# Batch 1's first transform step: pairs of pieces on 64x64 parts of the array, at other places of batch 0's group steps

## The chip, the cores and the metric

The kernel runs on one core of one Trainium2 chip. The metric is the device time of one execution in microseconds (us); three executions of the kernel before are given, and one more was profiled.

## The reference

The input `x` has 8 batches of 3008 tokens with 256 channels. Every batch goes through a spectral filter along its tokens (a real transform, a product with a complex filter, the transform back), and the result through a SwiGLU block with 1536 hidden units.

```python
X = np.fft.rfft(x, axis=1)
y = np.fft.irfft(X * (filt_r + 1j * filt_i)[None], n=x.shape[1], axis=1)
z = y.reshape(8 * 3008, 256)
g = z @ w_gate
out = (g * (1.0 / (1.0 + np.exp(-g))) * (z @ w_val)) @ w_out
```

All arrays here are 32-bit floats; the weights arrive as 64-bit floats and are rounded to 32 bits by the kernel itself while batch 0 is worked on.

## The kernel before

**The transform.** 3008 is 47 times 64, and the filter is worked out in steps of short transforms: over 47 values (`N1`), of which 24 complex outputs (`NS`) are kept, and over 64 (`N2`). The first step of batch 1 is the method `stage1` of the class `Spectral`. It works on 16 pieces (`N_ONE`) of `NV` = 2 token columns. A piece holds, on 94 partitions, the 47 rows of each of two halves (`h` = 0 and 1, token 32h + n of every row of 64), interleaved; the table `wf_t` (94 x 96) does both halves in one matmul, with zeros where the halves would mix. So a piece is one matmul of 94 x 96 on 512 columns into a PSUM bank, one copy by ScalarE (ACT) into a tile `t1`, and one store from the ACT queue into the DRAM tile `d1`, from which the next step (`stage2a`, first loads in `load_two`) reads. The inputs are loaded by `load_x` from SyncE's queue (SP), two DMAs a piece (80 and 14 rows), into the pool `xp` with two buffers: the first two pieces are loaded ahead, and piece u + 2 is asked for right after the matmul of piece u. `t1` has two buffers as well.

**Banks.** Of the eight PSUM banks, one belongs to the pool `fps` (function `fbank`), seven to `wps` (`NB` = 7, function `bank`). The group steps below take their accumulators from `wps`; `stage1` of batch 1 takes `fps` alone. A new `wps` tile gets the bank that was released first; its first writer waits until the last reader of the tenant before has ended.

**The group steps.** A batch is 12 steps (4 chunks of tokens by 3 groups of hidden units). Each step is one `Group`, and runs through one list of about 230 tokens, `SCHEDULE`, written out by hand; every instruction keeps this program order on its engine. Tokens such as `Q0` or `A13` are matmul pairs into the banks `k0` to `k3`, `a..` and `e..` (in the profile `wk`, `wa`, `we`; `W` tokens are the output products, `wA`, `wF`, `wG`). `f`, `c`, `m`, `g`, `u` are ACT's, `s`, `x`, `y`, `e`, `l`, `h`, `v` are mostly VectorE's (DVE) with some of ACT, `D` and `S` GpSimd's (POOL). A token with `'` belongs to the step before.

**Where the pieces go.** A token `tN.M` calls `next` once on entry N of the step's list `plan[step]`; a piece that is a generator runs to its next `yield`. The parts of the list that matter here:

```python
Q0 o3' z1.o' t4.2' W2 b0 f0 S00' S01' ... t0.0 x1.o' i1 Q1 t0.1 x2.o' P3 x3.o' f1 t4.3'
W1 x4.o' S10' x03 S11' D01 ... s13 b3 x5.o' P1 o1 b4 t0.2 P0 o2 z0.o c1 i5 A13 ...
... B01 h13 o7 t1.3 t2.0 s02 s12 g01 h2 b5 Q3 t2.1 h01 e12 A02 y23 W4 e02 ... A12 o4 z2.o t2.2 E12
... u13 E23 t3.2 m03 v13 E01 l23 e03 t3.3 t4.0 l01 u23 B23 v23 u01 E03 n1 t4.1 v01 g23 B03
```

Before the change `plan[0]`, `plan[1]` and `plan[2]` hold the four `stage3` pieces of batch 0 and one `stage1` piece each, at `t4`; `plan[3]` and `plan[4]` hold five pieces each, `plan[5]` three. Steps 6 to 10 hold `stage2a` and `stage2b` of batch 1. In steps 0 to 9 the rounding of the weights (`Preparation`, called `preparation.tick`) runs at further places between the tokens, on DVE, ACT and POOL.

In the profiled execution steps 0 to 5 lie at about 75 to 260 us. A step's `t4` is near its end, `t0` soon after its start, `t2` in its middle.

Of the kernel before, what the change touches and what calls it, by code (L numbers as in the profile page):

```python
# [41 lines left out]
FP32 = mybir.dt.float32  # L42
# [6 lines left out]
B, S, C = 8, 3008, 256  # L49
# [4 lines left out]
N1, N2 = 47, 64  # L54
# [71 lines left out]
def dft_tables():  # L126
    n1, n2 = np.arange(N1), np.arange(N2)
    s, q = np.arange(NS), np.arange(NQ)
    ph = 2 * np.pi * (np.outer(n1, s) % N1) / N1
    w = np.stack([np.cos(ph), -np.sin(ph)], 1)  # L130
    wf = np.zeros((N1, 2, NS, 2, 2))
    wi = np.zeros((NS, 2, 2, N1, 2))

    v = np.stack([2 * np.cos(ph), -2 * np.sin(ph)], 0)
    v[0, :, 0], v[1, :, 0] = 1.0, 0.0
    for h in range(2):
        wf[:, h, :, :, h] = w.transpose(0, 2, 1)
        wi[:, :, h, :, h] = v.transpose(2, 0, 1) / S
    one = wi[:, :, 0, :, 0].transpose(1, 0, 2).reshape(2 * NS, N1)
    back = np.zeros((128, 10 * N1))  # L140
    for tile_, first in zip(BACK, BACK_AT):
        for i, (_, row, a, rows) in enumerate(tile_):
            back[row:row + rows, first + N1 * i:first + N1 * (i + 1)] = one[a:a + rows]


    kap = np.where(q[:, None] < 32, s + N1 * q[:, None], s + N1 * (95 - q[:, None]))
    sg = np.where(q < 32, 1.0, -1.0)[:, None]
    th = 2 * np.pi * ((n2[:, None, None] * kap) % S) / S
    c, sn = np.cos(th), np.sin(th)
    d = np.zeros((2, N2, NS, 2, NQ))  # L150
    d[0, :, :, 0] = c.transpose(0, 2, 1)
    d[1, :, :, 0] = sn.transpose(0, 2, 1)
    d[0, :, :, 1] = (-sn * sg).transpose(0, 2, 1)
    d[1, :, :, 1] = (c * sg).transpose(0, 2, 1)
    d = d.reshape(128, NS, 128)
    chunks = np.arange(128).reshape(2, 2, NCHUNK, NW).transpose(2, 0, 1, 3).ravel()
    de = np.stack([d, d.transpose(2, 1, 0)[:, :, chunks]], 2)

    hi = 2 * np.pi * (np.outer(2 * n1 + 1, s) % (2 * N1)) / (2 * N1)
    scale = np.where(s == 0, 1.0, 2.0) / S  # L160
    one_hi = np.concatenate([np.cos(hi) * scale, -np.sin(hi) * scale * (s > 0)], 1).T
    for tile_, first in zip(BACK, BACK_AT):
        for i, (n, row, a, rows) in enumerate(tile_):
            if n >= NH:
                back[row:row + rows, first + N1 * i:first + N1 * (i + 1)] = one_hi[a:a + rows]

    quad = np.zeros((4, 32, 2, 32))
    for h in range(2):
        turn = 2 * np.pi * (np.outer(2 * n1[0:NS] + h, s) % (2 * N1)) / (2 * N1)
        quad[2 * h:2 * h + 2, 0:NS, 0, 0:NS], quad[2 * h:2 * h + 2, 0:NS, 1, 0:NS] = np.cos(turn), -np.sin(turn)  # L170
        quad[2 * h:2 * h + 2, 23 * h] *= np.array([0.5, 0.0])[:, None]
    quad = np.concatenate([quad.reshape(128, 64), np.tile([[1.0], [-1.0]], (64, 1))], 1)

    four = np.zeros((128, N_FOUR + 1, 2, 4, 64))
    lo, qq = np.arange(32), np.arange(32)
    for t in range(NS):
        u, at = divmod(t, 4)
        for e in range(2):
            qa = np.where(qq < 16, 2 * qq, 62 - 2 * (qq - 16)) + e
            ang = 2 * np.pi * (np.outer(lo, t + N1 * qa) % S) / S  # L180
            cs, sn, sign = np.cos(ang), np.sin(ang), np.where(qa < 32, 1.0, -1.0)
            there = np.stack([np.stack([cs, -sn * sign], 2), np.stack([sn, cs * sign], 2)], 0)
            part = 64 * (at // 2)
            four[part:part + 64, u, 0, at % 2 * 2 + e] = there.reshape(64, 64)
            home = np.stack([np.stack([cs.T, sn.T], 2),
                             np.stack([-(sn * sign).T, (cs * sign).T], 2)], 1)
            four[64 * e:64 * e + 64, u + 1, 1, at] = home.reshape(64, 64)
    four = four.reshape(128, N_FOUR + 1, 2, 256)

    thc = th - np.where(n2 < 32, 0.0, 1.0)[:, None, None] * 2 * np.pi * s / (2 * N1)  # L190
    c, sn = np.cos(thc), np.sin(thc)
    turned = np.zeros((2, N2, NS, 2, NQ))
    turned[0, :, :, 0] = c.transpose(0, 2, 1)
    turned[1, :, :, 0] = sn.transpose(0, 2, 1)
    turned[0, :, :, 1] = (-sn * sg).transpose(0, 2, 1)
    turned[1, :, :, 1] = (c * sg).transpose(0, 2, 1)
    turned = turned.reshape(128, NS, 128).transpose(2, 1, 0)

    pairs = np.arange(128).reshape(2, N2).T.ravel()
    later = np.stack([de[:, :, 0], turned[:, :, pairs]], 2)  # L200
    f32 = np.float32
    return (wf.reshape(NR, NK).astype(f32), wi.reshape(NK, NR).astype(f32),
            back.astype(f32), quad.astype(f32), four.astype(f32), np.ascontiguousarray(de).astype(f32),
            np.ascontiguousarray(later).astype(f32))


# [1 line left out]
def kernel(  # L208
# [8 lines left out]
    out: bass.AP,  # L217
):
    nc = tc.nc
    wf_host, wi_host, back_host, quad_host, four_host, de_host, later_host = dft_tables()  # L220
    wf_dram = nc.inline_tensor(wf_host, name="wf_tbl")
    wi_dram = nc.inline_tensor(wi_host, name="wi_tbl")
    quad_dram = nc.inline_tensor(quad_host, name="quad_tbl")
    four_dram = nc.inline_tensor(four_host, name="four_tbl").ap()
    back_dram = nc.inline_tensor(back_host, name="back_tbl")
    de_dram = nc.inline_tensor(de_host, name="de_tbl").ap()
    later_dram = nc.inline_tensor(later_host, name="later_tbl").ap()
# [14 lines left out]

    wf_t = cpool.tile([NR, NK], FP32)
    wi_t = cpool.tile([NK, NR], FP32)

    wt_t = cpool.tile([128, NPR, 2, 128], FP32)
    y_t = cpool.tile([128, 3 * len(PAIRS), TQ], FP32)
# [32 lines left out]
    f_dram = wdpool.tile([128, 2, NS, C], FP32, name="filter")  # L280
    wo_t = cpool.tile([128, NJ, 7, 128], FP32)

    off_t = cpool.tile([128, 1], FP32)
    top_t = cpool.tile([128, 1], FP32)
    one = cpool.tile([128, 1], FP32)
    nc.vector.memset(off_t, -896.0)
    nc.vector.memset(top_t, 255.0)

# [303 lines left out]
    class Spectral:  # L592


        def __init__(self, b):
            self.b = b
            self.quads_dram, self.turned = quads_dram[b % 2], turned_dram[b % 2]
            self.d1, self.d2 = [dram_tiles[2 * (b % 2) + i] for i in range(2)]
            self.d1_rows = self.d1.rearrange("a (h n) c -> (a h) n c", h=2)

            self.d2_tokens = self.d2.rearrange("a n c -> (a n) c").rearrange(
                "(n a) c -> n a c", n=N2)
            flat = self.d2.rearrange("a n c -> (a n) c")
            self.d2_parts = flat.rearrange("(s q) c -> q s c", q=128)
            self.d2_rows = flat.rearrange("(s k a n) c -> k s a n c", k=NCHUNK, a=4, n=NW)
            self.rest = []
            self.x, self.t2, self.f, self.tb, self.p, self.t4, self.y = {}, {}, {}, {}, {}, {}, {}
            self.real = {}
# [13 lines left out]
        def load_x(self, u):  # L622
# [15 lines left out]
                        self.load(out=up[ts(n, 32)].rearrange("p (q c) -> p q c", c=C),  # L638
                                  in_=rows[0:32, first:first + 4])
            elif u < N_ONE:  # L640
                self.x[u] = xpool.tile([NR, NV, C], FP32, name=f"x_{self.b}_{u}", tag="x")
                rows = x[self.b].rearrange("(r n) c -> r n c", n=32)

                for r in (slice(0, 80), slice(80, NR)):
                    self.load(out=self.x[u][r], in_=rows[r, ts(u, NV), :])

        def load_two(self, u):
            if u < N_TWO:
# [249 lines left out]
                self.f.pop(w)  # L898
            self.load_filter(w + 1)

        def stage1(self, u):

            t1 = t1pool.tile([NK, NV, C], FP32, name=f"t1_{self.b}_{u}", tag="t1", bufs=2)
            ps = self.bank(f"pa_{self.b}_{u}")
            pin(nc.tensor.matmul(out=ps[0:NK], lhsT=wf_t, rhs=self.x.pop(u),  # L905
                                         start=True, stop=True))
            self.load_x(u + 2)
            yield
            pin(nc.scalar.copy(out=t1, in_=ps[0:NK]))
            pin(nc.scalar.dma_start(out=self.d1_rows[:, ts(u, NV), :], in_=t1))  # L910

        def stage1_first(self, u):

# [332 lines left out]
    def run(piece):  # L1246
        for _ in piece:
            pass

    with tc.tile_pool(name="start", bufs=1) as spool0:  # L1250
# [88 lines left out]
        idle(zero, [bank("idle") for _ in range(6)], 512)  # L1339
        for step in (0, 2, 1, 3):  # L1340
            run(spec.stage3(0, step))
        following = Spectral(1)
        for u in range(2):
            following.load_x(u)
# [86 lines left out]
    for b in range(B):  # L1431
# [5 lines left out]
            return [s.stage3(k, step) for step in range(4)]  # L1437

        d = [three(cur, k) for k in range(1, NCHUNK)]
        one = [] if b else [nxt.stage1(u) for u in range(N_ONE)]  # L1440
        bursts = [[] for _ in range(NCHUNK * NG)]
        if b and nxt:
            for n in range(N_QUAD // 2):
# [10 lines left out]
        if nxt:  # L1454
# [3 lines left out]
            plan[4], plan[7], plan[11] = d[1], [gap] + d[2], three(nxt, 0)  # L1458
            if b == 0:
                for k in range(NCHUNK - 1):  # L1460
                    plan[k] = d[k] + one[k:k + 1]
                plan[0] = [gap, d[0][0], chain(d[0][1], d[0][2]), d[0][3], one[0]]
                plan[3], plan[4], plan[5] = one[3:8], one[8:13], one[13:16]
                for n in range(5):
                    plan[6 + n] = two[5 * n:5 * n + 5]
                plan[6][0] = sooner(plan[6][0])
# [105 lines left out]
```

## Time and profile before

| what | value |
|---|---|
| median of 3 runs | 2815.08 us (2807.47 to 2815.55) |
| the profiled execution's own time | 2812.9 us |
| its span, first to last instruction | 2811.1 us |
| mean granted TensorE clock | 0.998 |
| PE (matmuls) busy | 2774.9 us, 99% |
| DVE, ACT, POOL busy | 2050.7, 1560.3 and 1580.6 us |
| matmul records of `stage1` of batch 1 (`pa`) | 32 for 16 matmuls, 590 to 595 ns each, from 100.5 to 248.2 us |
| its copies (`t<-pa`) | 16, 563 to 589 ns |
| its stores (`d<-t`) on the ACT queue | 16, 310 to 361 ns of that queue each |

How to read it: a matmul of 32-bit floats shows as two records of the whole width. PE is the matmul, PEld the load of its stationary operand, which lies beside it. Records overlap, so that the time which a matmul takes from its neighbours is the distance from its start to the start of what follows. A queue's DMA instruction (SPq, ACTq) is the time that the queue spends on issuing, not the transfer.

### The profile page before, as it was taken

How to read it: one execution, taken by the hardware profiler on the slowest of the kernel's cores; microseconds unless marked ns; L12 is line 12 of the kernel's file. 1: busy time of each engine (PE TensorE's matmuls, PEld its weight loads, DVE VectorE, ACT ScalarE, POOL GpSimd, SP SyncE). 2: the span in 40 equal slices, each digit the busy share in tenths (PEclk: the TensorE clock that was granted, in tenths of full speed). 3: DMA queues.
4: the chain of work that ended last, by engine and by line, in shares of the span. 5: the costliest groups of instructions: out<-in, count | busy, mean ns of one | idle time of the engine just before them, and what ended most of it. 6: DMA issues, size and time to landing. Idle time of an engine off the chain costs nothing.

```text
span 2811.1 us, 49259 instructions
## 1 busy us (share of the span) xinstructions
PE 2774.9 (99%) x15828; PEld 2310.4 (82%) x15828; DVE 2050.7 (73%) x4675; ACT 1560.3 (56%) x4170; POOL 1580.6 (56%) x1689
## 2 busy tenths in 40 slices
PE   8999999999999999999999999999999999999998
PEld 6877888788888888888888888888888888888887
DVE  7888767767677767777767677777677767666666
ACT  5775455555555555555555555555555555555554
POOL 5886576465545565456654566455555455545544
PEclk9999999999999999999999999999999999999999
DMA  9778877877676776677767776668766677654543
GB/s 215 234 262 278 286 237 233 261 233 268 187 214 207 249 243 193 206 233 227 245 187 227 217 247 221 204 193 257 243 209 204 212 237 229 190 153 147 153 138 82
DMA packets 385273, 608.53 MB, mean 216 GB/s; under 512 B 198877, under 2 KB 268445, under 8 KB 384841
## 3 DMA queue, kind: packets, MB, share of 16 engines
q1 hardware_dynamic: 366202, 574.39, 65.0%
q10 hardware_dynamic: 16174, 25.50, 3.5%
q0 software_dynamic: 2640, 5.51, 0.8%
q8 instruction: 128, 2.10, 0.3%
q14 instruction: 129, 1.05, 0.1%
HBM read 484.65 MB, written 118.12 MB: 214 GB/s over the span
## 4 chain that ended last, share of the span: by engine, by line
PE 91%; DVE 3%; POOL 2%; ACT 1%; DMA 1%; issue 0%; SPq 0%; POOLq 0%; ACTq 0%; DVEq 0%
PE wa L1123 25%; PE wk L1123 17%; PE wA L1220 17%; PE we L1123 12%; PE wG L1220 8%; PE wF L1220 4%; PE pd L1026 3%; PE wqc L823 1%; PE wqb L835 1%; PE wqa L743 1%; POOL h L323 0%; POOL out_dram L1205 0%; DMA lent<-later_tbl 0%; PE pc L980 0%; PE pa L905 0%
## 5 line engine op out<-in xcount | busy, mean ns | idle before, releaser
L1123 PE MATMUL wa<-y_t,wt_t 128*128 128x188 f32 x4464 | 882.4, 324 | 6.3 <-DVE wa L1145 4.6
L1123 PEld LDWEIGHTS wa<-y_t,wt_t 128*128 128x128 f32 x4464 | 748.4, 190 | 85.1 <-ACT wa L1149 9.5
L1123 PEld LDWEIGHTS wk<-y,wt_t 128*128 128x128 f32 x2976 | 494.6, 190 | 113.9 <-issue 34.0
L1123 PE MATMUL wk<-y,wt_t 128*128 128x188 f32 x2976 | 577.2, 326 | 1.8 <-ACT f L1138 1.3
L320 POOL TENSOR_TENSOR h<-h 128x376 f32<-128x376 f32 x190 | 182.7, 982 | 686.8 <-DVE h L1170 686.8
L323 POOL TENSOR_TENSOR h<-h 128x376 f32<-128x376 f32 x572 | 559.4, 999 | 15.4 <-DVE h L320 15.2
L1220 PE MATMUL wA<-h,wo_t 128*128 128x376 f32 x1532 | 550.6, 481 | 5.7 <-DVE o L320 2.1
L1123 PE MATMUL we<-y_t,wt_t 128*128 128x188 f32 x2232 | 433.0, 323 | 2.2 <-ACT we L1154 1.5
L323 POOL TENSOR_TENSOR D<-f,f 128x376 f32<-128x376 f32 x288 | 281.2, 987 | 246.4 <-ACT f L1138 231.2
L323 DVE TENSOR_TENSOR we<-we,m 128x376 f32<-128x376 f32 x576 | 319.2, 555 | 126.1 <-PE we L1123 60.7
L1123 PEld LDWEIGHTS we<-y_t,wt_t 128*128 128x128 f32 x2232 | 368.6, 190 | 6.2 <-DVE we L327 3.9
L1220 PEld LDWEIGHTS wA<-h,wo_t 128*128 128x128 f32 x1532 | 275.8, 190 | 113.5 <-POOL h L323 5.1
L1158 ACT COPY m<-wa 128x376 f32<-128x376 f32 x576 | 272.2, 473 | 84.1 <-PE wa L1123 80.1
L1165 ACT ACTIVATE u<-we 128x188 f32<-128x188 f32 x576 | 188.6, 327 | 173.0 <-DVE we L323 165.6
L1165 ACT ACTIVATE g<-wa 128x188 f32<-128x188 f32 x576 | 187.2, 325 | 165.0 <-PE wa L1123 157.5
L327 DVE SCALAR_TENSOR_TENSOR y<-wk,c 128x376 f32<-128x376 f32 x480 | 246.1, 539 | 40.5 <-ACT c L1142 23.0
L1220 PE MATMUL wG<-h,wo_t 128*128 128x376 f32 x768 | 274.0, 479 | 0.0
L1142 ACT COPY c<-wk 128x376 f32<-128x376 f32 x288 | 136.3, 473 | 212.7 <-PE wk L1123 212.6
L1154 ACT COPY we<-y 128x376 f32<-128x376 f32 x480 | 222.1, 480 | 18.8 <-DVE h L1170 14.0
L1138 ACT ACTIVATE f<-wk 128x376 f32<-128x376 f32 x288 | 139.8, 486 | 165.2 <-PE wk L1123 130.6
L1170 DVE TENSOR_TENSOR h<-wa,g 128x188 f32<-128x188 f32 x576 | 198.7, 346 | 34.4 <-ACT g L1165 34.2
L1170 DVE TENSOR_TENSOR h<-we,u 128x188 f32<-128x188 f32 x576 | 198.1, 344 | 29.0 <-ACT u L1165 17.6
(193 smaller groups left out, 3561.4 us busy)
## 6 DMA issues: line engine op xcount, KB each, us to landing
wt_t<-w_all SPq DMA_DIRECT2D x174, 896.0 KB
wt_t<-w_all SPq DMA_DIRECT2D x174, 768.0 KB
lent<-filter SPq DMA_DIRECT2D x36, 1024.0 KB
quads<-lent SPq DMA_DIRECT2D x96, 256.0 KB
d<-lent ACTq DMA_DIRECT2D x84, 256.0 KB
lent<-quads SPq DMA_DIRECT2D x144, 128.0 KB
lent<-raw SPq DMA_DIRECT2D x144, 128.0 KB
t<-d SPq DMA_DIRECT2D x114, 128.0 KB
```

The lines of the kernel that those rows point to most:

```text
L320: return eng.tensor_tensor(out=dst, in0=a, in1=b, op=ALU.add)
L323: return eng.tensor_tensor(out=dst, in0=a, in1=b, op=ALU.subtract)
L327: return nc.vector.scalar_tensor_tensor(out=dst, in0=a, scalar=-1.0, in1=b, op0=ALU.mult, op1=ALU.subtract)
L1026: pin(nc.tensor.matmul(out=rows, lhsT=self.t4[k, i][:, j, ts(cb, 128)], rhs=cols, start=j == 0, stop=True, skip_group_check=True))
L1123: pin(nc.tensor.matmul(out=ps[:, z], lhsT=self.wt[:, SLOT[p], z], rhs=rhs, start=start and z == 0, stop=True, skip_group_check=True))
L1138: pin(act.mul(self.small(f"f{i}", f"f{i}", 1), t[f"k{i}"], -1.0))
L1142: pin(act.copy(out=self.small(f"c{i}", f"c{i}", 1), in_=t[f"k{i}"]))
L1154: pin(act.copy(out=self.bank(f"e{at}"), in_=t[f"y{at}"]))
L1158: pin(act.copy(out=self.small(f"m{at}", "m", 4), in_=t[f"a{at}"]))
L1165: pin(act.activation(out=self.small(op, "g", 3, 1)[:, 0], in_=ps[:, 1], func=AF.Silu))
L1170: pin(v.tensor_tensor(out=dst, in0=ps[:, 0], in1=g, op=ALU.mult))
L1220: pin(nc.tensor.matmul(out=self.tiles[at], lhsT=wo_t[:, JB * q + i, WO[p], :], rhs=self.hs[i][:, HID[p]], start=start and i == 0, stop=Tru ...
```

## The change

Batch 1's `stage1` is called for 8 pairs v of pieces, 2v and 2v + 1. Half h of a piece lies on partitions 64h to 64h + 47 of a 128-partition tile (48 rows loaded, 47 used), two loads of 48 rows a piece. A table `both_t` (2 x 47 rows of 64 columns) replaces `wf_t` there. Each piece and half is a matmul of 47 x 64 on 512 columns on one quarter of the array: the half sets the rows of the array and the bank, the piece sets the columns and so the half of the bank's partitions. The pair's half 0 goes to the `fps` bank, its half 1 to a bank of `wps`. ACT copies both banks (128 x 512) in one part of the generator, and the four stores of 48 rows follow in a third part. The loads of the two pieces after next follow the four matmuls. The pairs are at `t4` of steps 1 and 2 (their stores at `t4.2'` of the step after) and at `t0` and `t2` of steps 3, 4 and 5; step 0 has none. `both_t` is loaded once from SP before the first loads of batch 1, and three one-column tiles become columns of one tile.

```diff
@@ load_x
-                self.x[u] = xpool.tile([NR, NV, C], FP32, name=f"x_{self.b}_{u}", tag="x")
-                rows = x[self.b].rearrange("(r n) c -> r n c", n=32)
-
-                for r in (slice(0, 80), slice(80, NR)):
-                    self.load(out=self.x[u][r], in_=rows[r, ts(u, NV), :])
+                self.x[u] = xpool.tile([128, NV, C], FP32, name=f"x_{self.b}_{u}", tag="x")
+                xb = x[self.b]
+                for h in range(2):
+                    self.load(out=self.x[u][64 * h:64 * h + 2 * NS],
+                              in_=bass.AP(tensor=xb.tensor, ap=[[N2 * C, 2 * NS], [1, NV * C]],
+                                          offset=xb.offset + (32 * h + NV * u) * C))
@@ stage1
-        def stage1(self, u):
-            t1 = t1pool.tile([NK, NV, C], FP32, name=f"t1_{self.b}_{u}", tag="t1", bufs=2)
-            ps = self.bank(f"pa_{self.b}_{u}")
-            pin(nc.tensor.matmul(out=ps[0:NK], lhsT=wf_t, rhs=self.x.pop(u),
-                                         start=True, stop=True))
-            self.load_x(u + 2)
-            yield
-            pin(nc.scalar.copy(out=t1, in_=ps[0:NK]))
-            pin(nc.scalar.dma_start(out=self.d1_rows[:, ts(u, NV), :], in_=t1))
+        def stage1(self, v):
+            pieces = (2 * v, 2 * v + 1)
+            banks = [fbank(f"pa_{v}_0"), bank(f"pa_{v}_1").rearrange("p (n c) -> p n c", c=C)]
+            parts = [self.x.pop(u) for u in pieces]
+            for i, t in enumerate(parts):
+                for h in range(2):
+                    r = slice(64 * h, 64 * h + N1)
+                    pin(nc.tensor.matmul(out=banks[h][64 * i:64 * i + 64], lhsT=both_t[r],
+                                         rhs=t[r], start=True, stop=True))
+            for u in pieces:
+                self.load_x(u + 2)
+            yield
+            t1 = [t1pool.tile([128, NV, C], FP32, name=f"t1_{v}_{h}", tag="t1", bufs=2)
+                  for h in range(2)]
+            for h in range(2):
+                pin(nc.scalar.copy(out=t1[h], in_=banks[h]))
+            yield
+            for i, u in enumerate(pieces):
+                for h in range(2):
+                    at = 32 * h + NV * u
+                    pin(nc.scalar.dma_start(out=self.d1[:, at:at + NV],
+                                            in_=t1[h][64 * i:64 * i + 2 * NS]))
@@ the places
-        one = [] if b else [nxt.stage1(u) for u in range(N_ONE)]
+        one = [] if b else [nxt.stage1(v) for v in range(N_ONE // 2)]
...
-                    plan[k] = d[k] + one[k:k + 1]
-                plan[0] = [gap, d[0][0], chain(d[0][1], d[0][2]), d[0][3], one[0]]
-                plan[3], plan[4], plan[5] = one[3:8], one[8:13], one[13:16]
+                    plan[k] = d[k] + (one[k - 1:k] if k else [])
+                plan[0] = [gap, d[0][0], chain(d[0][1], d[0][2]), d[0][3]]
+                for k in range(3):
+                    plan[3 + k] = [one[2 + 2 * k], gap, one[3 + 2 * k]]
```

More of the change, by code (lines that the diff above doesn't have):

```diff
@@ L165, in dft_tables @@
                 back[row:row + rows, first + N1 * i:first + N1 * (i + 1)] = one_hi[a:a + rows]
+    both = np.zeros((2, 64, 64))
+    both[:, 0:N1, 0:2 * NS] = w.transpose(0, 2, 1).reshape(N1, 2 * NS)
+    both = both.reshape(128, 64)
     quad = np.zeros((4, 32, 2, 32))
@@ L202, in dft_tables @@
     return (wf.reshape(NR, NK).astype(f32), wi.reshape(NK, NR).astype(f32),
-            back.astype(f32), quad.astype(f32), four.astype(f32), np.ascontiguousarray(de).astype(f32),
+            both.astype(f32), back.astype(f32), quad.astype(f32), four.astype(f32), np.ascontiguousarray(de).astype(f32),
             np.ascontiguousarray(later).astype(f32))
@@ L219 @@
     nc = tc.nc
-    wf_host, wi_host, back_host, quad_host, four_host, de_host, later_host = dft_tables()
+    wf_host, wi_host, both_host, back_host, quad_host, four_host, de_host, later_host = dft_tables()
     wf_dram = nc.inline_tensor(wf_host, name="wf_tbl")
@@ L224 @@
     four_dram = nc.inline_tensor(four_host, name="four_tbl").ap()
+    both_dram = nc.inline_tensor(both_host, name="both_tbl")
     back_dram = nc.inline_tensor(back_host, name="back_tbl")
@@ L244 @@
     wi_t = cpool.tile([NK, NR], FP32)
+    both_t = cpool.tile([128, 64], FP32)
     wt_t = cpool.tile([128, NPR, 2, 128], FP32)
@@ L281 @@
     wo_t = cpool.tile([128, NJ, 7, 128], FP32)
-    off_t = cpool.tile([128, 1], FP32)
-    top_t = cpool.tile([128, 1], FP32)
-    one = cpool.tile([128, 1], FP32)
+    single = cpool.tile([128, 3], FP32)
+    off_t, top_t, one = [single[:, i:i + 1] for i in range(3)]
     nc.vector.memset(off_t, -896.0)
@@ L598, in __init__ @@
             self.d1, self.d2 = [dram_tiles[2 * (b % 2) + i] for i in range(2)]
-            self.d1_rows = self.d1.rearrange("a (h n) c -> (a h) n c", h=2)
             self.d2_tokens = self.d2.rearrange("a n c -> (a n) c").rearrange(
@@ L1341 @@
             run(spec.stage3(0, step))
+        pin(nc.sync.dma_start(out=both_t, in_=both_dram.ap()))
         following = Spectral(1)
```

## The prediction

> **What bounds the kernel.** I read the page's busy line and chain first:
>
> ```profile
> PE 2774.9 (99%) x15828; PEld 2310.4 (82%) x15828; DVE 2050.7 (73%) x4675; ACT 1560.3 (56%) x4170; POOL 1580.6 (56%) x1689
> PE 91%; DVE 3%; POOL 2%; ACT 1%; DMA 1%; issue 0%; SPq 0%; POOLq 0%; ACTq 0%; DVEq 0%
> ```
>
> TensorE is the bound of the whole, so what its queue is spared is worth its own time, wherever nothing else is late. Whether that holds in the touched stretch needs the windows view there (stretch, its us, then busy us and instructions of PE, PEld, DVE, ACT, POOL, then clock, DMA share, GB/s); the cuts are about those of steps 2, 3, 4 and 5:
>
> ```profile
> 135.00:166.00 31.00, 28.21 (x151) 22.85 (x150) 28.50 (x55) 20.99 (x60) 30.48 (x40) 1.00 0.73 248
> 166.00:197.00 31.00, 30.58 (x143) 23.36 (x143) 27.47 (x64) 25.25 (x70) 22.07 (x34) 1.00 0.87 290
> 197.00:227.00 30.00, 30.00 (x144) 23.73 (x143) 26.13 (x58) 20.79 (x56) 17.80 (x25) 1.00 0.87 293
> 227.00:263.00 36.00, 33.18 (x157) 25.33 (x156) 28.33 (x63) 21.49 (x59) 24.04 (x30) 1.00 0.78 269
> ```
>
> Steps 3 and 4 are PE's alone. In step 2 PE stands still for 2.8 us while DVE works 28.5 of 31 (weights are being rounded there), in step 5 for 2.8: there DVE and POOL set the pace. The DMA engines are 0.87 busy in steps 3 and 4.
>
> The timeline of PE at the end of step 2 shows one old piece (start, us, engine, line, tiles, shapes, count):
>
> ```profile
> 165.40 1.02 PE L905 MATMUL pa<-x,wf_t 94*96 94x512 f32 x2
> 166.26 0.80 PE L1123 MATMUL wa<-y_t,wt_t 128*128 128x188 f32 x4
> ...
> 168.17 1.43 PE L1220 MATMUL wG<-h,wo_t 128*128 128x376 f32 x4
> 169.44 0.80 PE L1123 MATMUL wk<-y,lent 128*128 128x188 f32 x4
> ```
>
> Start to start, the piece takes 166.26 - 165.40 = 0.86 us, with no loss on either side. Sixteen take 13.8 us. A `wG` record takes 1.27/4 = 0.317.
>
> **What the Trainium skill says.** "TensorEngine Tiling (Array Packing)", section Key Properties: tiles work in parallel, but changing the tiling mode drains the array. "TensorE: Matmul & The Clock Gate", Part 3: matmuls on different tiles overlap, at about 4 ns a tile. This trace has such a burst, batch 2's `wqb`, in the same order of rows and columns as the new pair (8 matmuls of 64x64 on 256 columns, 16 records):
>
> ```profile
> 561.25 1.43 PE L1220 MATMUL wF<-h,wo_t 128*128 128x376 f32 x4
> 562.60 1.09 PE L835 MATMUL wqb<-lent 64*64 64x256 f32 x16
> 563.62 1.07 PE L1026 MATMUL pd<-back,t 128*128 128x141 f32 x6
> ```
>
> It agrees with both pages. The four `wF` are over at 561.25 + 4 x 0.317 = 562.52, `wqb` starts 0.09 later, and the next work 1.02 after that: 1.11 us. Sixteen records of 256 columns, one by one at the old piece's 0.43 us for 512, would be 16 x 0.215 = 3.4; in fours they are 0.86. The remaining 0.25 is the price of going to 64x64 and back. The Tiling page's Gotcha 1 asks for different banks for different row tiles; the change does that.
>
> **Part by part.** *TensorE.* A pair is 4 matmuls, 8 records of 512 columns: in fours, 2 x 0.43 + 0.25 = 1.11 us against 2 x 0.86 = 1.72. Sum: 8 x 1.11 - 16 x 0.86 = -4.9 us. By place: step 0 -0.86, steps 1 and 2 +0.25 each, 3 and 4 -2.1 each, 5 -0.4. Bounds: full overlap as in `wqb` (-4.9); none between the two halves, 8 x 1.97 (+2.0).
>
> *The `wps` bank.* At `t0` several banks have been free for 2 to 4 us and the pair gives its own back before `k2` needs it: 0. At `t2` the `e12` and `e02` copies move to banks freed one place later: 0.3 in all (0 to 2.5, if step 5's late DVE sets it). At `t4` the next bank to come free is that of `e13`, whose last reader is `v13` on DVE. In step 1 that is over as PE arrives. In step 2 it is this:
>
> ```profile
> 166.42 0.34 DVE L1170 TENSOR_TENSOR h<-we,u 128x188 f32<-128x188 f32 x1
> ```
>
> It ends at 166.76, and PE is there at 165.40. The pair's second matmul waits 1.4 us, and B23, E03, B03, W3 and the next step's Q0 stand behind it, with DVE and ACT waiting for their banks. I take 1.4 (0 to 1.6; not below nothing, since a wait frees no work).
>
> *`t1` buffers.* Two tiles, both used by every pair. Only from step 2 to step 3 are pairs close: the first one's stores at `t4.2'` leave ACT at about 172 to 173, and the next pair's copies stand at about 174.5. The store's landing is not in the trace; other stores from ACT and SP to the same kind of tile land in 3.2 to 5.6 us (3.4 in the middle). So the copies wait until 176 to 178. Behind them on ACT is `f1`, for which P1 on PE waits:
>
> ```profile
> 174.07 0.31 ACTq L910 DMA_DIRECT2D d<-t  x1
> ...
> 174.85 0.46 ACT L1138 ACTIVATE f<-wk 128x376 f32<-128x376 f32 x1
> ```
>
> PE has Q1, P3 and W1 in between (2.5 us) and comes late anyway through the bank. I take 1.0 (0 to 2.4).
>
> *Loads.* Four SP issues of about 0.4 us a pair replace four for two pieces, the same bytes. Only pair 2 asks for its inputs late: they are issued after pair 1's matmuls, about 168 to 169.5, and wanted at about 173; loads of `x` land in 3.3 to 5.9 us. 0.3 (0 to 1.5). SP holds the reload of `y_t` behind them, which is wanted a third of a step later: 0, and at worst 1. `both_t` is one more SP issue among the first loads of batch 1, which lie 25 us ahead of need; the joined small tiles cost nothing.
>
> *ACT.* Copies stay 16. Stores grow from 16 to 32, at 0.31 us of the queue: +5.0 us on an engine that is 56% busy, but in fours (1.24 us), and with two copies (1.17) ahead of `f1` or `e12`. In steps 4 and 5 W1 (1.27 us) covers the later `f1`; `f0`, `c1` and `m12` move. 0.1 a pair: 0.8 (0 to 3).
>
> *What others take back.* Step 0 and 1 gain 0.6 before step 2, where DVE sets the pace; step 5 gains 0.4 under DVE and POOL. 0.5 of it is lost (0 to 1.2). The last stores come a token later (`t2.2`), before batch 1's second step reads `d1` from SP: its first load has 8 us to its use (256.17 to 264.62), so 0 (0 to 2).
>
> Sum: -4.9 + 0.3 + 1.4 + 1.0 + 0.3 + 0.8 + 0.5 = -0.6 us. The profiled execution took 2812.9 (span 2811.1), so 2812.3; the median of the runs shown stands 2.2 above that execution, so I forecast **2814.5**: no change. A measurement of this kernel can tell about 0.3%, 8.4 us, from no change.
>
> **The rivals.** *A, the whole gain arrives*: the waits at step 2 fall into what PE loses there anyway (2.8 us idle), and the `t1` wait is covered: -4.2 us, 2810.9. For it: PE is full in steps 3 and 4. Against: `v13` is plainly late. Still within 0.3%.
>
> *B, the bursts hold up the queues: slower.* Place: ACT's queue at every `t0.2`, `t2.2` and `t4.2'`. Four stores in a row, each allowed out only as earlier transfers finish, stop ACT with `c1`, `m12` or `f0` behind them, and PE behind those. The view of SP's own waits shows that SP already stops for these stores (waiting line and what for, us in total, times, longest):
>
> ```profile
> SPq L611 <- DMA d<-t: 8.8, 5, 2.4
> SPq L1196 <- DMA d<-t: 3.5, 1, 3.5
> ```
>
> and the DMA engines are nearly full in steps 3 and 4. Against: ACT's 16 old stores each start within 0.05 us of their copy's end, so ACT itself never stopped. At 1.8 us a pair in place of 0.1 the sum is -0.6 + 8 x 1.7 = +13: 2828. It passes 8.4 from 1.2 us a pair on.
>
> *C, the quarters do not overlap*: +2.0 in place of -4.9: 2821.4, within 0.3%. Against it: the `wqb` burst.
>
> **How the numbers follow.** Forecast 0.60, A 0.18, B 0.16, C 0.06. Range: the best bound is 2810.2, from which the runs shown scatter down by up to 8; the upper bounds of banks, `t1`, loads and ACT together (-4.9 + 2.5 + 1.6 + 2.4 + 2.5 + 3 + 1.2 + 2 = +10.3) give 2825. I take 2807 to 2824, which leaves out most of B. Faster by over 0.3% needs more than all of PE's gain: 0.04, for scatter alone. Slower by over 0.3%: B and a little of the upper bounds, 0.17. Same 0.79.
>
> **What would show it.** `pa` matmuls: 64 records in bursts of eight, about 1.11 us to the next work (else C). At step 2's `t4` the second matmul about 1.4 us after the first, with a wait on DVE; in step 3 ACT's first `t<-pa` waiting for a DMA `d<-t`. PE's busy time down by some 5 us, its idle time in steps 2 and 3 up by 2 to 3. If ACT's stores start late in every burst, B is right. Wrong altogether would be a change outside 75 to 265 us.

## The result and the profile after

The changed kernel takes 2821.71 us (median of 14 runs, 2818.57 to 2826.08), the kernel before 2815.32 in the same job (14 runs, 2807.47 to 2817.4). The ratio is 1.0027, 95% interval 1.0019 to 1.0034: slower by some 7 us. That is less than the 0.3% that the prediction called the limit of a measurement, but more than these runs are uncertain by, and on the other side of nought from the forecast of -0.6 us. The profiled execution took 2822.33, its span is 2820.6; the one before had a span of 2811.1.

The busy line and the chain of the page after, the same two lines as were shown of before:

```profile
PE 2778.0 (98%) x15860; PEld 2311.2 (82%) x15860; DVE 2047.7 (73%) x4675; ACT 1559.8 (55%) x4170; POOL 1581.6 (56%) x1689
PE 89%; POOL 3%; DVE 2%; ACT 1%; DMA 1%; issue 1%; ACTq 0%; SPq 0%; POOLq 0%; DVEq 0%
```

TensorE should have been busy some 5 us less; it is busy 3.1 us more, and its share of the chain falls from 91 to 89%. Where it happens is seen in the windows view, cut as before (stretch, its us, then busy us and instructions of PE, PEld, DVE, ACT, POOL, then granted clock, DMA share, GB/s):

```profile
135.00:166.00 31.00, 28.23 (x152) 23.06 (x150) 28.68 (x56) 21.29 (x60) 30.53 (x40) 1.00 0.81 263
166.00:197.00 31.00, 26.90 (x123) 19.64 (x123) 21.91 (x48) 20.05 (x54) 21.04 (x31) 0.89 0.69 216
197.00:227.00 30.00, 29.56 (x155) 22.90 (x154) 25.67 (x59) 21.06 (x58) 18.46 (x28) 1.00 0.86 292
227.00:263.00 36.00, 31.27 (x153) 22.10 (x152) 26.75 (x56) 19.45 (x52) 24.26 (x31) 1.00 0.84 286
```

The second line is step 3. It was PE's alone (30.58 us busy of 31, 143 instructions); now 123 instructions get through, PE stands still for 4.1 us, and the mean granted clock is 0.89 where it was 1.00. The last line, step 5, has 1.9 us less of PE too; but the cuts are fixed in time and the work stands some 7 us later here, so that figure alone proves nothing.

The timeline of PE from the end of step 2 (start, us, engine, line, tiles, shapes, count; in brackets the idle time ahead and what ended it):

```profile
166.00 1.07 PE L914 MATMUL pa<-x,both_t 47*64 47x512 f32 x2
167.32 0.64 PE L914 MATMUL wpa<-x,both_t 47*64 47x512 f32 x1 [0.25 <-DVE h L1188]
...
168.33 0.90 PE L1141 MATMUL wa<-y_t,wt_t 128*128 128x188 f32 x4
...
173.60 0.64 PE L914 MATMUL pa<-x,both_t 47*64 47x512 f32 x1
...
174.62 1.54 PE L1141 MATMUL wk<-y,lent 128*128 128x188 f32 x8
176.00 1.43 PE L1238 MATMUL wA<-h,wo_t 128*128 128x376 f32 x4
181.28 1.93 PE L1141 MATMUL wk<-y,lent 128*128 128x188 f32 x5 [3.86 <-ACT f L1156]
```

Three things are to be read. An undisturbed pair (173.60) takes 1.02 us to the next work: the quarters do overlap. In step 2 half 1 (`wpa`) comes 167.32 - 166.00 = 1.32 us after half 0: the bank. And in step 3 P1 (the last line) starts only at 181.28, because `f1` on ACT is late. The bracket counts from the modelled end of the record ahead; from where the four `wA` are over at full rate (176.00 + 4 x 0.317 = 177.27) PE stands for 4.0 us. Stops of PE are given this second way below, 0.16 us more than in the brackets. The DVE instruction behind the first wait is `v13`, as before, ending at 166.93 + 0.34 = 167.27:

```profile
166.93 0.34 DVE L1188 TENSOR_TENSOR h<-we,u 128x188 f32<-128x188 f32 x1
```

ACT's timeline says why `f1` is late:

```profile
170.67 0.31 ACTq L927 DMA_DIRECT2D d<-t  x1
...
171.02 1.56 ACTq L927 DMA_DIRECT2D d<-t  x3
...
179.22 0.58 ACT L922 COPY t<-pa 128x512 f32<-128x512 f32 x1 [5.13 <-DMA d<-t]
...
180.75 0.47 ACT L1156 ACTIVATE f<-wk 128x376 f32<-128x376 f32 x1
```

The four stores of step 2's pair are issued from 170.67 to 172.58. The copies of step 3's first pair need the same two `t1` tiles and stand 5.13 us, until 179.22, 6.6 us after the last of those issues. `f1` is behind them. SP stops for stores of this kind as well (the view of its own waits from 95 to 260 us: line, what for, us in total, times, longest):

```profile
SPq L615 <- DMA d<-t: 17.8, 7, 5.8
SPq L386 <- DMA d<-t: 0.9, 1, 0.9
```

The first of these lines had 8.8 us before, but there more lines waited. Over all lines of the view it is 18.7 us here and 17.6 before, so that SP is hardly held up more than it was.

To put sizes on the places, take the start of each TensorE instruction that both kernels have and subtract the two traces. The table gives the median of that difference over the instructions that start within 2 us of a time of the kernel before; the difference makes a step at 255.2, and column 255 is its level behind that step, up to 257 (us; one trace of each kernel; the starting offsets up to 160 us are scatter of the first stage, between -2.2 and +5.4 in single executions, so only the steps along a line count):

| kernel | 160 | 168 | 172 | 182 | 245 | 255 | 500 |
|---|---|---|---|---|---|---|---|
| changed | 0.51 | 2.17 | 1.98 | 7.39 | 6.49 | 8.76 | 8.56 |
| early | 1.19 | 1.17 | 1.04 | 2.26 | 1.36 | 3.64 | 2.87 |
| spread | 0.45 | 2.12 | 0.71 | 1.39 | 3.50 | 6.11 | 5.39 |
| SP stores | -2.16 | -0.49 | -0.69 | 3.24 | -0.06 | 0.43 | 2.81 |
| early, SP stores | -0.03 | 0.00 | -0.17 | -1.40 | -4.39 | -3.17 | -3.27 |
| spread, SP stores | 0.09 | 1.75 | 0.34 | 1.02 | 0.43 | 0.90 | 0.09 |
| places alone | 5.35 | 6.84 | 7.15 | 11.11 | 9.82 | 10.88 | 11.38 |
| early, spread, SP | 1.32 | 1.35 | -0.03 | 1.72 | -0.35 | 0.14 | -1.20 |

The changed kernel loses at three places: step 2 (160 to 168), the start of step 3 (172 to 182), and step 5's second pair (245 to 255). The other lines are experiments, told below.

### The profile page after: what moved, and what is told of

Its sections match the earlier page's. It is cut to its first block, busy times and chain, and to the rows that moved or that the text cites. A ratio compares the mean times of both kernels' runs of the same rounds, so it can differ in the third digit from the quotient of the medians.

```text
span 2820.6 us, 49341 instructions
## 1 busy us (share of the span) xinstructions
PE 2778.0 (98%) x15860; PEld 2311.2 (82%) x15860; DVE 2047.7 (73%) x4675; ACT 1559.8 (55%) x4170; POOL 1581.6 (56%) x1689
## 4 chain that ended last, share of the span: by engine, by line
PE 89%; POOL 3%; DVE 2%; ACT 1%; DMA 1%; issue 1%; ACTq 0%; SPq 0%; POOLq 0%; DVEq 0%
PE wa L1141 24%; PE wk L1141 16%; PE wA L1238 16%; PE we L1141 12%; PE wG L1238 8%; PE wF L1238 4%; PE pd L1044 3%; PE wqc L828 1%; PE wqb L840 1%; PE wqa L748 1%; POOL h L328 1%; POOL y_t L325 0%; POOL out_dram L1223 0%; DMA lent<-later_tbl 0%; PE pc L998 0%
## 5 line engine op out<-in xcount | busy, mean ns | idle before, releaser
L332 DVE SCALAR_TENSOR_TENSOR y<-wk,c 128x376 f32<-128x376 f32 x480 | 246.0, 538 | 43.2 <-ACT c L1160 25.0
L1172 ACT COPY we<-y 128x376 f32<-128x376 f32 x480 | 221.8, 480 | 17.6 <-DVE h L1188 13.9
```

The source lines that it names most:

```text
L332: return nc.vector.scalar_tensor_tensor(out=dst, in0=a, scalar=-1.0, in1=b, op0=ALU.mult, op1=ALU.subtract)
L1172: pin(act.copy(out=self.bank(f"e{at}"), in_=t[f"y{at}"]))
```

## The experiments

Two theories stood at the start. **T**: the pairs of steps 2 and 3 are too close for two `t1` tiles, so ACT's copies, `f1` and P1 wait, and PE's clock is halved after it. **B**, the prediction's rival: bursts of four stores in ACT's queue cost something at every pair. After the first four runs they became one, **S**: both are true, at different places. In each row below the ratio is to the kernel before in the same job, with its 95% interval; "us" is that ratio less 1, times the median of before. The intervals reach 2 to 4 us to either side, so the tenths of these figures are not to be relied on; where something is lost is read from the traces.

### First two pairs a step earlier (e1_early)

```
-  plan[k] = d[k] + (one[k - 1:k] if k else [])
+  plan[k] = d[k] + (one[k:k + 1] if k < 2 else [])
-  plan[0] = [gap, d[0][0], chain(d[0][1], d[0][2]), d[0][3]]
+  plan[0] = [gap, d[0][0], chain(d[0][1], d[0][2]), d[0][3], one[0]]
```

> The first two pairs stand at t4 of steps 0 and 1 in place of steps 1 and 2, the other six as in the changed kernel. So no pair lies within a step of another until step 3. Theory T (the t1 buffers of step 2's pair hold up step 3's f1, PE stands 4.0 us and runs 1.8 us longer at half clock; the bank wait of step 2 is another 1.3): both go, 5.7 + 1.3 = 7.0 us off 2821.7: 2814 to 2816. In the trace no gap of PE over 3 us in step 3, and no clock of 0.5 there. Theory B (four stores in a row hold up ACT's queue in every burst): the count of bursts is the same, so 2820 to 2822.

Measured: 2815.97, ratio 1.0007 (0.9999 to 1.0015), +2.0 us: 5.6 us better than the changed kernel, as T has it, and inside T's range. No copy waits, and P1 comes on time, right behind W1. But a new stop, of 2.3 us, opens further on in step 3, at P2. The timelines of ACT and PE of this kernel (`f1`, P1, the stores, `f2`, P2):

```profile
175.49 0.48 ACT L1156 ACTIVATE f<-wk 128x376 f32<-128x376 f32 x1
176.32 1.44 PE L1141 MATMUL wk<-y,lent 128*128 128x188 f32 x8
...
177.57 2.60 ACTq L927 DMA_DIRECT2D d<-t  x3
...
182.12 0.53 ACT L1156 ACTIVATE f<-wk 128x376 f32<-128x376 f32 x1
...
182.70 0.90 PE L1141 MATMUL wk<-y,lent 128*128 128x188 f32 x4 [2.18 <-ACT f L1156]
```

Now it is this pair's own stores that hold ACT's queue, the last three of them for 2.6 us, with `c1`, `m13` and `f2` behind them. B is true here: with the stores on SP's queue as well (below) this stop is gone. No clock of 0.5 follows.

### Step 3's pairs at t1 and t3 (e2_spread)

```
+  plan[3] = [gap, one[2], gap, one[3]]
```

> Only step 3 is changed: its pairs stand at t1 and t3 in place of t0 and t2, a third of a step further from step 2's pair. Theory T: the stores of step 2's pair land before the copies of step 3's first pair, so P1 of step 3 does not wait and the clock stays: 5 to 6 us off 2821.7, so 2815.5 to 2817; the bank wait of 1.3 us in step 2 stays. Theory B: unchanged, 2821 to 2822.

Measured: 2821.03, ratio 1.0027 (1.0018 to 1.0037): no different from the changed kernel. T alone is refuted by it. P1 does come on time (172 to 182: +0.7 in place of +5.4), and the bank wait of step 2 is given back at once (168 to 172: -1.4). But between 182 and 245 a new loss comes, and its line is again a store on ACT's queue:

```profile
184.24 3.43 ACTq L927 DMA_DIRECT2D d<-t  x2
187.72 0.33 ACT L1183 ACTIVATE g<-wa 128x188 f32<-128x188 f32 x1 [3.27 <-DMA d<-t]
...
189.64 0.91 PE L1141 MATMUL wa<-y_t,lent 128*128 128x188 f32 x4 [3.09 <-ACT wa L1167]
```

The program gives each DMA of SP and ACT one of eight completion semaphores in turn, and an issue waits until the DMA eight before it is over. The fourth store here waits for a 752 KB transfer that SP issued at 180.01: that one is over at 187.34, and the store is issued at 187.37. A burst of stores runs into whatever large transfer is eight back.

### Stores from SP's queue (e3_sp_stores)

```
-  pin(nc.scalar.dma_start(out=self.d1[:, at:at + NV],
+  pin(nc.sync.dma_start(out=self.d1[:, at:at + NV],
   ...
```

> As the changed kernel, but the four stores of a pair are issued from SP's queue in place of ACT's. Theory B: ACT is free of the stores, 2813 to 2816. Theory T: the copies of step 3's first pair still wait for the same stores to land (a little later, since SP has loads ahead of them), so 2820 to 2824, with the wait of P1 in step 3 still 4 us or more.

Measured: 2817.61, ratio 1.0009 (1.0002 to 1.0016), +2.5 us: 5.1 better than the changed kernel, between the two expectations. The copies' wait of 4.87 us for `d<-t` is still there, PE still stands 3.6 us before P1 (172 to 182: +3.9). What is gone is most of step 5's loss (245 to 255: +0.5 in place of +2.3), and some 2.4 us between 182 and 245 (-3.3 in place of -0.9). Step 5 in the changed kernel, ACT then PE:

```profile
260.11 0.33 ACT L1183 ACTIVATE g<-wk 128x188 f32<-128x188 f32 x1 [0.27 <-DVE y L332]
260.18 1.90 ACTq L927 DMA_DIRECT2D d<-t  x4
262.12 0.47 ACT L1176 COPY m<-wa 128x376 f32<-128x376 f32 x1 [1.68 <-PE we L1141]
...
262.64 0.90 PE L1141 MATMUL wa<-y_t,lent 128*128 128x188 f32 x4 [1.20 <-ACT m L1176]
```

and the same place with the stores on SP:

```profile
253.57 0.33 ACT L1183 ACTIVATE g<-wk 128x188 f32<-128x188 f32 x1 [0.27 <-DVE y L332]
253.79 0.47 ACT L1176 COPY m<-wa 128x376 f32<-128x376 f32 x1
```

From `g` to `m` it is 2.01 us with the burst between them and 0.22 without. The bracket names PE as what `m` waited for, but PE had long been done: `m` stood behind the stores.

### Two pairs close in step 4 as well (e4_close)

```
+  plan[4] = [one[4], one[5], gap]
```

> As the changed kernel, but step 4's pairs stand at t0 and t1 in place of t0 and t2: a second place where two pairs follow within a third of a step. Theory T: a second wait of ACT's copies for a DMA d<-t, and PE behind it: 2 to 5 us more than 2821.7, so 2824 to 2827. Theory B: the same bursts, 2821 to 2822.

Measured: 2823.8, ratio 1.0034 (1.0022 to 1.0047), +9.6 us. The interval reaches over the changed kernel's, so this doesn't tell the theories apart. Nor did the trace show what T said: step 4's second pair lost time to a late load, not to a `t1` tile (PE's timeline):

```profile
214.16 0.61 PE L914 MATMUL wpa<-x,both_t 47*64 47x512 f32 x1 [0.67 <-DMA x<-in_x_dram]
```

### Half the store instructions (e5, e6, e7)

On the changed kernel, the early one and the spread one:

```
-  for i, u in enumerate(pieces):
-      for h in range(2):
-          at = 32 * h + NV * u
-          pin(nc.scalar.dma_start(out=self.d1[:, at:at + NV], in_=t1[h][64 * i:64 * i + 2 * NS]))
+  for h in range(2):
+      at = 32 * h + 2 * NV * v
+      pin(nc.scalar.dma_start(
+          out=self.d1_all[:, at:at + 2 * NV].rearrange("a (i n) c -> i a n c", i=2), in_=t1[h]))
```

(`d1_all` is `d1` with 64 rows.)

> As the changed kernel, but a pair's intermediates leave in two stores of 128 rows (16 of each 64 are zeros) in place of four of 48: the same eight places, half the store instructions, a third more bytes. The theory that has grown out of the first runs, S: beside the t1 wait, the four stores in ACT's queue themselves cost PE, 2.3 us at step 5 and 2.3 to 3.3 us in step 3 wherever the t1 wait is taken away. S: the wait of ACT's copies in step 3 for d<-t stays near 5 us (the same stores, landing no sooner), step 5 loses under 1 us in place of 2.3: 2819 to 2821. If stores in a queue cost nothing (T alone): 2821 to 2822.5. If it is the bytes that count: 2823 or more.

> First two pairs at t4 of steps 0 and 1, and two stores a pair. S: nothing waits for a t1 buffer, and half of what ACT's queue costs at step 3 (2.3) and step 5 (2.3) goes: 2 to 3 us below the early kernel's 2816, so 2813 to 2814. T alone: 2815 to 2816.5, as the early kernel.

> Step 3's pairs at t1 and t3, and two stores a pair. S: the wait of the fourth store in step 3 (3.3 us on ACT, for an eighth-last transfer of 752 KB) needs four stores in a row; with two it goes or shrinks to under 1 us, and step 5 loses under 1: 3 to 5 us below the spread kernel's 2821, so 2816 to 2818. T alone: 2820 to 2822.

Measured: 2878.96, 2862.2 and 2875.01, ratios 1.0228 (1.0214 to 1.0242), 1.0168 (1.0154 to 1.0182), 1.0213 (1.0199 to 1.0227): 47 to 64 us slower, far above what either theory allows; only the open end of the first text, "2823 or more" if it is the bytes that count, takes this in. So they say nothing on S, but they price what S rests on, a store that lands late. ACT's and PE's timelines of the first of them:

```profile
181.10 0.58 ACT L923 COPY t<-pa 128x512 f32<-128x512 f32 x1 [8.44 <-DMA d<-t]
188.08 0.58 ACT L923 COPY t<-wpa 128x512 f32<-128x512 f32 x1 [6.39 <-DMA d<-t]
...
189.49 2.87 PE L1142 MATMUL wk<-y,lent 128*128 128x188 f32 x8 [13.50 <-ACT f L1157]
```

The two stores were issued at 169.2 to 170.3 and land only at 181 and 188. Their DRAM side begins with a dimension of 2. In the trace their packets are at most 4 in flight (four stores of 48 rows in the changed kernel: up to 20), and each store ends with 2 completion packets where a store of 48 rows ends with 16: two DMA engines carry all 256 KB of it. That is what the Trainium skill says, "DMA: Bandwidth & Descriptors", section Why a DMA increments its semaphore by 16 and not by 1: a DMA is split over the largest number of engines up to 16 that divides the slowest dimension of both sides. Here that is 2; the trace agrees. Two stores a pair with a first dimension that is a multiple of 16 were not tried, so the third more bytes are not told apart from the two engines.

### Early, and stores from SP (e8_early_sp)

The edits of the first and the third experiment together.

> First two pairs at t4 of steps 0 and 1, and the four stores of a pair from SP's queue in place of ACT's. No t1 wait, no bank wait in step 2, no stores in ACT's queue. S: the early kernel's 2816 less the 2.3 of step 3 and the 2.3 of step 5: 2811 to 2813, if SP can carry the stores without a later load. If SP's loads become late behind the stores: 2815 or more, with waits of PE for x or y_t in steps 3 to 5.

Measured: 2810.61, ratio 0.9985 (0.9976 to 0.9993), -4.2 us: faster than both kernels, and just below what S expected. This completes a square: changed +7.6, early +2.0, SP stores +2.5, both -4.2. The early places are worth 5.6 with ACT's stores and 6.7 with SP's, SP's stores 5.1 and 6.2: within the intervals the two causes add up. Step 3 of this kernel is full again (windows view):

```profile
166.00:197.00 31.00, 30.34 (x160) 23.67 (x159) 29.25 (x68) 25.87 (x73) 22.39 (x34) 1.00 0.88 286
```

PE does 160 records there, 123 in the changed kernel. SP's own waits for `d<-t` are gone from the view of 95 to 260 us.

### Spread, and stores from SP (e9_spread_sp)

> Step 3's pairs at t1 and t3, and a pair's four stores from SP's queue. Against the kernel with SP stores alone (2817.6) only the t1 wait of step 3 is taken away (3.7 us on PE there), the bank wait of step 2 stays. S: 2812.5 to 2814.5, with no wait of ACT for d<-t, and not the 3.4 us hold of ACT's queue that the spread kernel had in step 3. If that hold moves to SP and so to PE's inputs: 2816 or more.

Measured: 2814.99, ratio 1.0009 (1.0001 to 1.0017), +2.5 us: just above S's range. Step 3 is as S said (172 to 182: +0.7), and no store holds ACT. But the `t1` wait has moved on, to where `t3` of step 3 now meets `t0` of step 4 (SP's and ACT's timelines):

```profile
192.20 0.58 ACT L922 COPY t<-pa 128x512 f32<-128x512 f32 x1
...
199.24 3.31 SPq L927 DMA_DIRECT2D d<-t  x4
...
206.28 0.59 ACT L922 COPY t<-pa 128x512 f32<-128x512 f32 x1 [3.62 <-DMA d<-t]
```

The copies are done at 193.3, SP gets to the stores only at 199.24, and the next pair, 11.4 us after the last on PE, finds its tiles in use; PE stands for 2.3 us before P1. So distance alone doesn't decide; when the stores are issued does.

### A control: the kernel before with stores from SP (e10_before_sp)

```
-  pin(nc.scalar.dma_start(out=self.d1_rows[:, ts(u, NV), :], in_=t1))
+  pin(nc.sync.dma_start(out=self.d1_rows[:, ts(u, NV), :], in_=t1))
```

> A control: the kernel before, with its 16 stores from SP's queue in place of ACT's. S: its single stores never held ACT up, so 2813.5 to 2815.5, no difference. If moving the stores to SP is a gain by itself, of about the 5 us that it gave the changed kernel: 2808 to 2811.

Measured: 2812.68, ratio 1.0 (0.9992 to 1.0009). Within some 2.5 us the single stores cost nothing on ACT's queue; the 5 us belong to the bursts.

### The places alone, with old pieces (e11_places)

The old loads come back as well; each place has two stores in a row.

```
-  for h in range(2):
-      r = slice(64 * h, 64 * h + N1)
-      pin(nc.tensor.matmul(out=banks[h][64 * i:64 * i + 64], lhsT=both_t[r], rhs=t[r], ...))
+  pin(nc.tensor.matmul(out=banks[i][0:NK], lhsT=wf_t, rhs=t, start=True, stop=True))
...
+  for i, u in enumerate(pieces):
+      pin(nc.scalar.dma_start(out=self.d1_rows[:, ts(u, NV), :], in_=t1[i][0:NK]))
```

> The places of the changed kernel (t4 of steps 1 and 2, t0 and t2 of steps 3 to 5), but at each of them two old pieces: two matmuls of 94x96, two copies and two stores of 96 rows. S: PE has none of its 4 to 5 us gain, the bank wait (1.6) and the t1 wait (3 to 5) of the places stay, the two stores cost about half of four: 2819 to 2823. If the 64x64 matmuls themselves and not the places cost the time: 2814 to 2816.

Measured: 2819.69, ratio 1.0020 (1.0013 to 1.0026), +5.6 us, in S's range. With TensorE's work as before, the places alone cost this: 1.5 at step 2, 4.0 in step 3 (172 to 182; the copies wait 4.7 us for `d<-t`). Step 5's second place, with two stores in the burst, loses 1.1 in place of 2.3.

### Early and spread, stores from SP (e12_early_spread_sp)

> First two pairs at t4 of steps 0 and 1, those of steps 3 and 4 at t1 and t3, step 5's at t0 and t2, all stores from SP. S: nothing is left of the three costs, as in the early kernel with SP stores (2810.6), and the shift of the e12 bank in steps 3 and 4 (0.4 us each) goes too: 2809 to 2811. If t1 and t3 are worse places for ACT or the banks: 2812 or more.

Measured: 2812.79, ratio 0.9995 (0.9987 to 1.0003), -1.4 us: a miss for S, by the same mechanism as in the spread kernel with SP stores. From `t3` of step 4 to `t0` of step 5 the copies wait 2.7 us for `d<-t` and PE stands 2.3 before P1. The early kernel with SP stores at `t0` and `t2` has the best ratio of all that ran, though its interval touches this one's.

## Why the prediction was wrong

*The bound and TensorE's term: right, a little too good.* A pair to the next work is 1.02 us, with 0.08 ahead of it (`wF` is over at 172.25 + 4 x 0.317 = 173.52): 1.10, as taken from `wqb`. (Within a group the starts lie 7 ns apart, in `wqb` as in the pairs, where the page that the prediction names has about 4; nothing here rests on it.) In the differences a pair nets +0.35 against one old piece, so 0.86 + 0.35 = 1.21 (the work just after it starts some 0.1 late). 8 x 1.21 - 16 x 0.86 = -4.1 in place of -4.9. Rival C is out. That the pairs bring this is seen in the early kernel with SP stores: -4.4 at 245.

*Bank in step 2: right.* 1.32 us, taken as 1.4, ended by `v13` as said; 0.4 of it is given back at `wF`, where the kernel before waited for DVE.

*The step that failed first: the `t1` term*, taken as 1.0 and bounded at 2.4. It cost 6.2 us. The place and the chain (copies, `f1`, P1) were as written; the size was not, in two ways. First, the landing of 3.2 to 5.6 us was taken from other stores; these tiles were released 6.6 us after the last issue. From the release to P1 it is 2.06 us (179.22 to 181.28), so that a stop of 1.0 from 177.27 on stands for a release at 176.2: it came 3.0 later. That the DMA engines were 0.93 busy at the end of that time and large transfers lay ahead is the likely reason, which no run tests by itself. P1 came 3.9 us later for it (5.92 us behind the kernel before, where it had been 1.98). Second, this had a price that no term held, put at nothing without a reason. The windows view of the changed kernel, the end of the stop and what follows:

```profile
176.66:180.07 3.41, 0.77 (x3) 0.16 (x1) 0.36 (x2) 0.79 (x2) 0.00 (x0) 1.00 0.93 353
180.10:186.90 6.80, 5.62 (x17) 5.51 (x18) 3.70 (x8) 4.87 (x14) 5.52 (x9) 0.50 0.84 266
```

The clock is 0.5 for 6.8 us, and the matmuls there take twice as long. By its end the difference has grown from 5.92 to 7.39, although an old piece of 0.86 has dropped out meanwhile: 1.47 + 0.86 = 2.3 us.

The Trainium skill has this in "TensorE: Matmul & The Clock Gate", Part 1: after an idle window of about 3.4 us the clock goes to half. The traces show the halving, but not that a stop must last so long. Here the clock fell at 180.07, 2.8 us into the stop. A stop of 3.26 us (spread kernel) left it at 1.00, and in the kernel before, which the prediction had, the clock fell to 0.5 at 81.75, inside a stop of 2.6 us of the first step:

```profile
83.02 2.85 PE L1123 MATMUL wa<-y_t,wt_t 128*128 128x188 f32 x8 [2.44 <-DVE wa L1145]
...
81.75:91.99 10.24, 8.72 (x29) 8.28 (x30) 8.63 (x21) 6.23 (x19) 5.81 (x11) 0.50 1.03 346
```

What the traces do show is a grid. In each of the fourteen traces all changes of the clock from 60 to 2790 us are whole multiples of 3.41 us apart. Cut each trace at these points: the clock fell at the end of all 39 stretches that began at full clock and had PE busy under 0.455 of the time (0.77 of 3.41 above), at the end of 10 of the 89 between 0.455 and 0.705, and of none of the other 10971. (PE's busy time is modelled at the ends of matmuls, so the shares are good to a few hundredths at best.) The spread kernel's stop fell on two stretches, 0.63 and 0.46 busy. A stop of 2.4 us, the prediction's bound, leaves a stretch 0.30 busy if it lies wholly inside (1.01 of 3.41), so the bound did not shut out the slower clock.

*The second: the ACT term*, 0.1 a pair, 0.8 in all, with the burst as a rival that was argued away. That each old store had started within 0.05 us of its copy was true, and the control bears it out, but it speaks of single stores. Between 182 and 245 us the changed kernel should gain 5 x 0.86 - 4 x 0.35 = 2.9 (five old pieces less, and four replaced by pairs). With early places and SP stores it gains 3.0, as it is only 0.9: 2.0 lost. In step 5 it is 1.8 (2.3 against the 0.5 with SP stores). Together 3.8, over the five pairs from step 3's second on 0.8 each. What step 3's first burst costs cannot be told apart here, as it lies in the stretch of half clock; between the early kernels with and without SP stores it is 2.5 us (172 to 182: +1.2 and -1.2). Rival B was right in mechanism, at under half of its price of 1.8 in the changed kernel.

*Loads: right for PE.* No pair of the changed kernel waits on PE for `x`, and SP's own waits for the stores hardly grew (17.6 to 18.7 us).

*What others take back: 0.5, measured 1.0.* Step 5's end should gain 0.86 - 0.35 = 0.5 and with SP stores loses 0.5; DVE and POOL set the pace there, as was said.

The sum again for the changed kernel, from 160 us on: PE 7 x 1.21 - 14 x 0.86 = -3.6, bank 1.3 - 0.4, `t1` and clock 6.2, ACT's queue 3.8, step 5 1.0: +8.3, where the traces differ by 8.56 - 0.51 = 8.05. The terms are read from the same traces, so this shows that little is left over, not that each is exact.

Two agreements are luck. The measured 2821.71 lies inside the stated range because the unused bounds on banks, loads and the last stores made up for two terms that broke theirs (6.2 and 3.8 against 2.4 and 3). And it is rival C's number, 2821.4, though C did not happen.

## What to carry to other kernels

When single transfers are bundled, ask of the burst what was never asked of one: what stands behind it in its queue, which transfer each of its issues waits for, and when its source tiles are free again; a queue whose engine sits on the path to the bound is the wrong place for it. Bound a landing by the slowest transfer in the same stretch at the same DMA load, and where a stall can leave the bound engine less than about half busy over some 3.4 us, price a slower clock too; the trace of before may show, as here, what stall was enough. Two causes at different places hide each other: taking one away alone (the spread kernel) moved nothing, a square of two by two showed both.

## What the runs showed that was not expected

- Two stores of 256 KB whose DRAM side starts with a dimension of 2 landed 11 and 18 us after their issue (step 2's pair), and kernels with such stores were 47 to 64 us slower; the last of four of 96 KB with a first dimension of 48 landed in about 7.
- The length of a stop of PE does not tell whether its clock falls: it fell with stops of 4.02 us (changed kernel), 3.60 (SP stores) and 1.7 (early kernel with SP stores, 242.6 to 246.0 us, where the next pair took 1.85 us in place of 1.02), and not with 3.26 (spread), 2.34 (early) or 2.26 (spread with SP stores). The busy share of PE between two points of a 3.41 us grid does, below 0.455 and above 0.705; what decides between these is open.
- Four stores in a row keep ACT's queue for 1.9 us where the profile shows no wait (step 5), and for up to 4.2 us (183.42 to 187.67, spread kernel) when the DMA eight before is a large one.
